# Gates of two batches made in one set of instructions, in an attention and mixture-of-experts kernel

## The chip, the cores and the metric

The kernel runs on one core of one Trainium2 chip. The metric is device time in microseconds (us), the median of several executions. The kernel before took 689.92 us in the median of three runs.

## What is computed

Two blocks, one behind the other. The first is attention with 8 batches, 8 heads, 576 positions and a head size of 64; heads 0 to 3 look at the last 32 positions, heads 4 to 7 at positions of the same class modulo 32. Its output, as rows `x` of 512 numbers (one for each of 8 x 576 positions), goes to a mixture of 8 experts. Each row is sent to one expert, and a gate decides which:

```
logits = np.einsum('bsd,de->bse', x, w_gate)
local_gate = 1.0 / (1.0 + np.exp(-np.einsum('bsd,de->bse', x, w_local).squeeze(-1)))
...
            fresh_e = int(np.argmax(logits[b, s]))
            if s == 0 or local_gate[b, s] < 0.5:
                e = fresh_e
            else:
                e = prev_e if prev_e >= 0 else fresh_e
            prev_e = e
            ls = logits[b, s] - logits[b, s].max()
            p = np.exp(ls)
            p /= p.sum() + 1e-09
            h = np.maximum(x[b, s] @ w1[e], 0.0)
            out[b, s] = p[e] * (h @ w2[e])
```

So each position needs nine numbers, 8 logits and the local gate, and from them a probability for each expert and a code that tells whether the expert is chosen afresh. All of it is in fp32.

## The kernel before, in words

The core has a matrix engine (TensorE, PE in the profile), a vector engine (VectorE, DVE), an activation engine (ScalarE, ACT), GpSimd (POOL) and SyncE (SP), which issues most of the DMAs. Each engine takes its instructions in the order of the program and waits on semaphores for others. [...] here the attention has three pools of PSUM tiles: `psS` (two tiles `sps`, for scores), `psV` (two tiles `vps`, for values and for gates) and `psT` (one tile `tps`, for transposes, for logits and for the router).

The order of the work is written out by hand in the loop at L433. Step `n` takes one pair of heads, in the order batch, pair (4 pairs a batch, so 32 pairs); a pair consists of two units. A step does, in this order: loads for four steps ahead (SP), scores and mask of pair n (L261, L265, L272), the store of finished rows of pair n-2 (L302), the transposes of pair n-2 (`turn_x`, L327), values and their normalizing for pair n-1 (L285, L298, L299), two of 16 weight sums for the first expert (L714, in steps 10 to 17, on DVE), and then what is due for whole batches. The last pair of batch b is number 4b+3; then

- `logits(b)` (L340) in step 4b+5: sixteen matmul records multiply the transposed rows by `wgs`, the weights of gate and local gate, padded to 32 columns. The four row blocks of 128 go to four strips of 32 rows of the tile `tps`, as four partial sums. Four copies (L351, L352, L354, L357) bring them to a tile `lT` of 128 partitions x 576 positions, two on ACT and two on DVE; the lower two also bring the positions of the strided heads back to their order. For batch 7 the engines of two copies change places and the tile is `sps`.
- `gates(b)` (L360) in step 4b+6: matmuls with a piece of `lT` as the stationary operand and `fold` as the moving one (L367) turn positions to partitions and add the four partial sums; there are 5 pieces, the last of 64 positions twice, so 6 matmuls, which the profile shows as 12 records. Thirteen small operations follow on 128 x 5 x 8 numbers (L372 to L392), all but one of them (L381, exp, on ACT) on DVE. They leave `codes` and `probs`.
- `store_p(b)` (L394) in step 4b+7: two DMAs from the POOL queue write the probabilities to DRAM beside the rows.

When four batches have their gates (step 19) the router for these starts: transposes of `codes`, scans on DVE (L547, L554), small matmuls (L559, L574) and a table. It takes one piece a step (`also[n]`), behind the gates in the same step. A gather of rows for the first expert is due in step 29. When the attention is done, the experts follow (L817, L853 and so on), to the end of the kernel; the change doesn't touch them.

Of the kernel before, what the change touches and what calls it, by code (L numbers as in the profile page):

```python
# [8 lines left out]
F32 = mybir.dt.float32  # L9
# [3 lines left out]
Alu = mybir.AluOpType  # L13
AX = mybir.AxisListType
# [4 lines left out]
P = 128  # L19
B, H, S, DH = 8, 8, 576, 64  # L20
D = H * DH
E, F = 8, 1024
DK, FK = D // P, F // P
# [14 lines left out]
PL, GC, GT = S // STRIDE, 7, 5  # L38
GR = STRIDE - GC * (GT - 1)
GK, GL = PL * GC, PL * GR  # L40
# [9 lines left out]
CH = -(-S // P)  # L50
RB = 4
# [7 lines left out]
WARM = 10  # L59

FILL = 4

ARMS = 7
SKIP = 8192
# [2 lines left out]
FRESH = -1.08674975e-07  # L67


def spread(ap, shape):  # L70

    dims = list("abcd"[:len(shape) - 1])
    left = " ".join(dims[:-1] + [f"({dims[-1]} o)"])
    right = " ".join(dims + ["o"])
    return ap.rearrange(f"{left} -> {right}", o=1).to_broadcast(shape)
# [7 lines left out]
def across(ap, shape):  # L83

    return ap.rearrange("a (o b) -> a o b", o=1).to_broadcast(shape)
# [60 lines left out]
def attention(ctx, tc, qkl, qks, vl, vs, wg, xd, ident, router, moe):  # L146

    nc = tc.nc
    sums, probs, codes = router.sums, router.probs, router.codes
    consts = ctx.enter_context(tc.tile_pool(name="consts", bufs=1))  # L150
# [4 lines left out]
    small = ctx.enter_context(tc.tile_pool(name="small", bufs=2))  # L155
# [4 lines left out]
    st = {}  # L160
# [18 lines left out]
    def busy(n):  # L179
        for _ in range(n):  # L180
            ps = psV.tile([P, 512], F32, name="vps")
            nc.tensor.matmul(ps, lhsT=warm[:, 0:P], rhs=warm, start=True, stop=True)  # L182

    busy(WARM)
    wgs = consts.tile([P, DK, 32], F32, name="wgs")
    nc.scalar.dma_start(out=wgs, in_=wg.rearrange("(k p) e -> p k e", p=P))

    identb = consts.tile([P, P], BF16, name="identb")
# [21 lines left out]
    for n, c in blocks:  # L210

        i, div = consts.tile([GK, 1], I32, name=f"row{n}"), consts.tile([GK, 1], F32, name=f"div{n}")
# [7 lines left out]
    n = GK  # L220
    nc.vector.tensor_copy(maskS[:, 0:2 * n].rearrange("p (a x) -> p a x", a=2), across(apart[n], [n, 2, n]))
    nc.vector.tensor_copy(maskS[:, 2 * n:], apart[GL])
    fold = consts.tile([P, E + 1], F32, name="fold")
    ci = consts.tile([P, E], I32, name="ci")
    down = consts.tile([P, E], F32, name="down")
    pi = consts.tile([P, CH], I32, name="pi")
    pos8 = consts.tile([P, CH], F32, name="pos8")
    start = consts.tile([P, CH], F32, name="start")

    def more_constants():  # L230

        nc.vector.tensor_reduce(fold, ident.rearrange("p (k x) -> p x k", k=DK)[:, 0:E + 1], axis=AX.X, op=Alu.add)


        nc.gpsimd.iota(ci, pattern=[[-1, E]], base=E, channel_multiplier=0)
        nc.vector.tensor_copy(down, ci)
        nc.gpsimd.iota(pi, pattern=[[E * P, CH]], base=E, channel_multiplier=E)
        nc.vector.tensor_copy(pos8, pi)
        nc.vector.tensor_scalar(start, pos8, float(E), None, Alu.is_equal)
# [100 lines left out]
    def logits(b):  # L340
        xT = st["xT", b]
        n = GK * (GT - 1)
        both = ((0, slice(0, n)), (1, slice(n, S)))
        final = b == B - 1

        ps = [psS.tile([P, 2, 512], F32, name="sps") for _ in range(2)] if final else [psT.tile([P, 2, 512], F32, name="tps")] * 2
        for kk, a, c in [(kk, *x) for kk in range(DK) for x in both] if final else [(kk, *x) for x in both for kk in range(DK)]:
            nc.tensor.matmul(ps[kk // 2][32 * kk:32 * kk + 32, a, 0:c.stop - c.start], lhsT=wgs[:, kk], rhs=xT[:, kk, c],  # L348
                             start=True, stop=True, skip_group_check=True)
        lT = small.tile([P, S], F32, name="lT")  # L350
        nc.scalar.copy(out=lT[0:64, 0:n], in_=ps[0][0:64, 0, 0:n])  # L351
        (nc.scalar.copy if final else nc.vector.tensor_copy)(out=lT[0:64, n:], in_=ps[0][0:64, 1, 0:GL])  # L352
        o = lT[64:].rearrange("p (y c) -> p y c", c=STRIDE)
        (nc.vector.tensor_copy if final else nc.scalar.copy)(  # L354
            out=o[:, :, 0:GC * (GT - 1)].rearrange("p y (j c) -> p j y c", c=GC),
            in_=ps[1][64:, 0, 0:n].rearrange("p (j y c) -> p j y c", j=GT - 1, c=GC))
        nc.vector.tensor_copy(o[:, :, GC * (GT - 1):], ps[1][64:, 1, 0:GL].rearrange("p (y c) -> p y c", c=GR))  # L357
        st["lT", b] = lT

    def gates(b):  # L360

        ps = psV.tile([P, 2, 3, V1], F32, name="vps").rearrange("p a i e -> p (a i e)")
        lt = ps[:, 0:CH * (E + 1)].rearrange("p (t e) -> p t e", e=E + 1)
        for t in range(CH):
            m = min(P, S - t * P)
            for o in range(0, P, m):
                nc.tensor.matmul(lt[o:o + m, t], lhsT=st["lT", b][:, t * P:t * P + m], rhs=fold,  # L367
                                 start=(t == 0), stop=True, skip_group_check=True)
        lg = lt[:, :, 0:E]
        shape = [P, CH, E]  # L370
        mx = small.tile([P, CH], F32, name="gmx")
        nc.vector.tensor_reduce(mx, lg, axis=AX.X, op=Alu.max)  # L372
        mxb = spread(mx, shape)
        ex = small.tile(shape, F32, name="ex")
        nc.vector.tensor_tensor(ex, lg, mxb, op=Alu.subtract)

        eq = small.tile(shape, F32, name="eq")
        nc.vector.tensor_tensor(eq, lg, mxb, op=Alu.is_equal)
        fr = small.tile([P, CH], F32, name="fr")
        nc.vector.scalar_tensor_tensor(fr, lt[:, :, E], FRESH, start, Alu.is_le, Alu.max)  # L380
        nc.scalar.activation(ex, ex, Act.Exp)  # L381
        nc.vector.tensor_tensor(eq, eq, across(down, shape), op=Alu.mult)
        code = small.tile([P, CH], F32, name="code")
        nc.vector.tensor_reduce(code, eq, axis=AX.X, op=Alu.max)
        nc.vector.tensor_tensor(code, pos8, code, op=Alu.subtract)

        nc.vector.tensor_tensor(codes[:, :, b], spread(code, shape), spread(fr, shape), op=Alu.mult)
        sm = small.tile([P, CH], F32, name="gsm")
        nc.vector.tensor_reduce(sm, ex, axis=AX.X, op=Alu.add)
        nc.vector.tensor_scalar(sm, sm, 1e-9, None, Alu.add)  # L390
        nc.vector.reciprocal(out=sm, in_=sm)
        nc.vector.tensor_tensor(probs[:, :, b, 0:E], ex, spread(sm, shape), op=Alu.mult)  # L392

    def store_p(b):  # L394
        dst = xd[b * S:(b + 1) * S, D:DX]
        full = S // P
        nc.gpsimd.dma_start(out=dst[0:full * P].rearrange("(t p) c -> p t c", p=P), in_=probs[:, 0:full, b])
        nc.gpsimd.dma_start(out=dst[full * P:], in_=probs[0:S - full * P, full, b])
# [19 lines left out]
    n = PAIRS * RB + 3  # L418
# [4 lines left out]
    m = n  # L423
# [9 lines left out]
    for n in range(len(units) + 3):  # L433
        if n < len(units):
            if n + ahead < len(order):
                load(*order[n + ahead])
            if 5 <= n < 13:
                moe.W[0].load(nc, moe.w1, moe.w2, 0, n - 5)
            if n == 10:
                steps = moe.W[0].sums(nc.vector)  # L440
            for u in units[n]:
                scores(u)
                mask(u)
        if 0 <= n - 2 < len(units) and order[n - 2][1] % 2 == 1:
            store_x(units[n - 2][1])
        if 0 <= n - 2 < len(units) and n != len(units):
            turn_x(*order[n - 2])
        if 0 <= n - 1 < len(units):
            for u in units[n - 1]:
                values(u)  # L450
                norm(u)
        if n == len(units):
            turn_x(*order[n - 2])
            moe.turn(moe.first, spare, 0)
        elif n == len(units) + 1:
            busy(FILL)
        for do in steps[:2]:
            do()
            steps.remove(do)
        for b in range(B):  # L460
            last = PAIRS * b + PAIRS - 1
            if n == last + 3:
                gates(b)
            if n == last + 4 and b < B - 1:
                store_p(b)
            if n == last + 2:
                logits(b)
        if n == len(units) + 1:
            moe.turn(moe.first, bank, 1)
            busy(2)  # L470
            moe.row_sums(moe.first)
        for do in also[n]:
            do()
# [1056 lines left out]
```

## Time and profile before

| | us |
|---|---|
| three timed runs | 687.54, 689.92, 690.97 |
| their median | 689.92 |
| the profiled execution | 686.27 |
| its span, first to last instruction | 684.5 |
| PE busy | 666.4 |
| DVE busy | 356.7 |
| ACT busy | 198.2 |

The attention ends and the first expert matmul begins at 165.0 us of the span. The granted clock of PE was 0.993 of full speed in the mean. A profile line of a group reads: line of the program, engine, operation, the tiles it writes and reads, shapes, count, then busy time, mean duration in ns, and the idle time of the engine just before with what ended it. A timeline line has start and duration first. A line of the chain of waits has start and duration and what the time went to. A line of the windows view has, for each stretch, its length, busy time and number of instructions of PE, PE's weight loads, DVE, ACT and POOL, then PE's granted clock, the share of the DMA engines and GB/s.

### The profile page before, as it was taken

To read this page: it belongs to the slowest core of one execution; us is meant where nothing else is said; L and a number is where in the kernel's file an instruction comes from. 1 tells how busy PE (TensorE), PEld (TensorE's weight loads), DVE (VectorE), ACT (ScalarE), POOL (GpSimd) and SP (SyncE) were. 2 spreads that over 40 slices of the span, in tenths; PEclk is the share of its full clock that TensorE was granted. 3 is DMA by queue.
4 is the path that set the end of the run, shared out by engine and by line. 5 is a ranking of instruction groups with operands and counts; after the bars stand their busy time and mean duration, and the time that the engine had idled before them with its cause. 6 is when DMAs were issued, how large, how long until landed. Compare 5 with 4: busy or idle time off the path is not lost.

```text
span 684.5 us, 14864 instructions
## 1 busy us (share of the span) xinstructions
PE 666.4 (97%) x6055; PEld 574.2 (84%) x6056; DVE 356.7 (52%) x821; ACT 198.2 (29%) x365; POOL 117.7 (17%) x144
## 2 busy tenths in 40 slices
PE   9999999999999999999999999999999999999994
PEld 6888887887998999589989999997799899699493
DVE  6558866865895437126532654651256546522131
ACT  3454453544312221222222122122222132221220
POOL 3440000012021113111111202202111113121001
PEclk9999999999999999999999999999999999999998
DMA  9999878733611172171236118111612622021001
GB/s 322 402 377 329 274 250 279 255 114 121 226 36 43 50 268 76 40 275 40 57 120 204 56 29 294 51 32 40 251 48 65 234 75 72 34 57 41 18 9 35
DMA packets 35800, 95.80 MB, mean 140 GB/s; under 512 B 4790, under 2 KB 11702, under 8 KB 35628
## 3 DMA queue, kind: packets, MB, share of 16 engines
q1 hardware_dynamic: 27164, 71.41, 29.6%
q0 software_dynamic: 7936, 22.38, 10.1%
q8 instruction: 66, 1.08, 0.6%
q14 instruction: 106, 0.87, 0.4%
q10 hardware_dynamic: 528, 0.07, 0.1%
HBM read 74.66 MB, written 19.69 MB: 138 GB/s over the span
## 4 chain that ended last, share of the span: by engine, by line
PE 93%; DVE 3%; issue 1%; ACT 1%; DMA 1%; POOL 0%; SPq 0%; DVEq 0%; POOLq 0%
PE lps L817 30%; PE mps L853 28%; PE sps L261 6%; PE vps L285 5%; PE lps L908 4%; PE mps L919 4%; PE tps L327 3%; PE xps L760 2%; PE mps L949 2%; PE lps L929 2%; PE sps L255 2%; PE vps L367 1%; PE tps L348 1%; DVE xl L299 1%; PE vps L182 1%
## 5 line engine op out<-in xcount | busy, mean ns | idle before, releaser
L773 POOL DMA_INDIRECT out_dram<-y,tab x40 | 46.1, 1153 | 351.4 <-DVE y L805 247.4
L817 PE MATMUL lps<-tt,ws 128*128 128x128 f32 x768 | 91.8, 275 | 0.3 <-issue 0.3
L817 PEld LDWEIGHTS lps<-tt,ws 128*128 128x128 f32 x768 | 88.6, 192 | 0.6 <-issue 0.5
L853 PE MATMUL mps<-wt,k 128*128 128x256 f32 x384 | 85.7, 380 | 0.0
L853 PEld LDWEIGHTS mps<-wt,k 128*128 128x128 f32 x384 | 72.8, 190 | 9.9
L817 PE MATMUL lps<-xt,w1t 128*128 128x128 f32 x512 | 63.2, 276 | 3.0 <-ACT y L955 1.9
L817 PEld LDWEIGHTS lps<-xt,w1t 128*128 128x128 f32 x512 | 60.4, 192 | 6.5 <-ACT y L955 3.7
L805 DVE TENSOR_TENSOR h<-lps,u 128x512 f32<-128x512 f32 x48 | 33.2, 691 | 58.3 <-PE lps L817 58.2
L853 PE MATMUL mps<-w2t,h 128*128 128x256 f32 x256 | 60.5, 379 | 0.0
L747 POOL DMA_INDIRECT x<-xd,gi x40 | 41.1, 1027 | 84.8 <-issue 34.7
L265 ACT ACTIVATE e<-sps 128x576 f32<-128x576 f32 (+1 forms) x64 | 41.3, 650 | 40.0 <-PE sps L261 39.2
L853 PEld LDWEIGHTS mps<-w2t,h 128*128 128x128 f32 x256 | 47.4, 190 | 5.8
L261 PE MATMUL sps<-qk 64*128 64x96 f32 (+2 forms) x704 | 51.2, 283 | 0.1
L804 ACT ACTIVATE h<-h 128x512 f32<-128x512 f32 x48 | 30.3, 630 | 70.1 <-DVE h L805 69.0
L261 PEld LDWEIGHTS sps<-qk 64*128 64x128 f32 (+2 forms) x704 | 43.1, 185 | 8.5 <-issue 7.2
L804 ACT ACTIVATE h<-lps 128x512 f32<-128x512 f32 (+1 forms) x28 | 15.7, 563 | 81.8 <-PE lps L817 65.6
L805 DVE TENSOR_TENSOR u<-lps,p 128x512 f32<-128x512 f32 x16 | 11.1, 691 | 52.5 <-PE lps L817 31.6
L753 ACT ACTIVATE x<-x 128x512 f32<-128x512 f32 (+1 forms) x40 | 27.1, 717 | 34.5 <-DMA x<-xd,gi 21.1
L761 ACT COPY xt<-xps 128x512 f32<-128x512 f32 (+1 forms) x38 | 20.3, 565 | 49.3 <-PE xps L760 49.3
L817 PE MATMUL lps<-xt,ws 128*128 128x128 f32 x256 | 31.3, 275 | 0.0
L817 PE MATMUL lps<-tt,w1t 128*128 128x128 f32 x256 | 31.3, 275 | 0.0
L853 PE MATMUL mps<-w2t,k 128*128 128x256 f32 x128 | 30.4, 380 | 0.0
(236 smaller groups left out, 974.5 us busy)
## 6 DMA issues: line engine op xcount, KB each, us to landing
w1t<-in_w_dram SPq DMA_DIRECT2D x7, 2048.0 KB
w2t<-in_w_dram SPq DMA_DIRECT2D x7, 2048.0 KB
qk<-in_qkl_dram SPq DMA_DIRECT2D x16, 592.0 KB
qk<-in_qks_dram SPq DMA_DIRECT2D x16, 576.0 KB
vl<-in_vf_dram SPq DMA_DIRECT2D x8, 780.0 KB
vs<-in_vg_dram SPq DMA_DIRECT2D x8, 639.8 KB
xd<-xl SPq DMA_DIRECT2D x12, 288.0 KB
xd<-xs SPq DMA_DIRECT2D x48, 63.0 KB
```

The costliest lines, as they stand in the source:

```text
L261: nc.tensor.matmul(ps[0:m, h, c:c + w], lhsT=t[r, S + j * width:S + j * width + m], rhs=t[r, j * width:j * width + w], start=(u.local and ...
L265: nc.scalar.activation(e[0:kb, :, 0:n], ps[0:kb, :, 0:n], Act.Exp, bias=0.0, scale=1.0 / DH ** 0.5)
L285: nc.tensor.matmul(ps[a * HALF:(a + 1) * HALF, h, i], lhsT=u.e[0:m, h, q0:q0 + HALF], rhs=vt[0:m, j, 2 * i2 + h], start=(i == 0 and h == 0 ...
L747: self.nc.gpsimd.indirect_dma_start(out=r.x[0:r.m, i], out_offset=None, in_=self.xd[0:r.rows], in_offset=bass.IndirectOffsetOnAxis(ap=r.gi ...
L753: self.nc.scalar.activation(r.x[0:r.m, i, 0:D], r.x[0:r.m, i, 0:D], Act.Copy, scale=r.gate[i][0:r.m])
L773: s = self.nc.gpsimd.indirect_dma_start(out=self.out, out_offset=bass.IndirectOffsetOnAxis(ap=r.si[i][0:r.m], axis=0), in_=y[0:r.m, i], in ...
L804: relu = lambda o, i: nc.scalar.activation(o, i, Act.Relu)
L805: add = lambda o, i, p: nc.vector.tensor_tensor(o, p, i, op=Alu.add)
L817: nc.tensor.matmul(ps[:, f], lhsT=m[:, kk, f * P:(f + 1) * P], rhs=v[:, kk], start=(start and f == 0 and kk == 0), stop=(kk == 1), skip_gr ...
L853: nc.tensor.matmul(ps[:, 0:256], lhsT=m[:, f], rhs=v[:, f], start=(start and f == 0), stop=(f == 3), skip_group_check=True)
L908: nc.tensor.matmul(ps[:, f], lhsT=w.w1[:, kk, c:c + P], rhs=r.xt[:, 0, kk], start=(f == 0 and kk == 0), stop=(kk == DK - 1), skip_group_ch ...
L919: nc.tensor.matmul(ps, lhsT=h[f // 4][:, f % 4], rhs=w.w2[:, f], start=(f == 0), stop=(f == FK - 1))
```

## The change

The gates of batches 0 and 1, 2 and 3, and 4 and 5 are made by one call each (`TWINS` is {1: 0, 3: 2, 5: 4}); batches 6 and 7 stay alone. For this the weights `wgs` get 16 columns of zeros ahead of them. The first of two batches uses columns 16 to 47, so its logits lie in rows 0 to 8 of each strip of 32, with zeros below; the second uses columns 0 to 31, so its logits lie in rows 16 to 24. Instead of copying the second's, four additions on DVE add them to the first's `lT` in place. `gates` is not called after the first of two; after the second it is called once, with 18 columns of `fold` for 9, and its small operations work on 80 numbers a partition for 40. Both batches' `store_p` come in the step behind it. The matmuls of `logits`, the copies of first and single batches and the places of the calls are as they were.

```diff
+TWINS = {b: b - 1 for b in range(1, B - 1, 2) if b % RB}
...
-    wgs = consts.tile([P, DK, 32], F32, name="wgs")
+    wgs = consts.tile([P, DK, 48], F32, name="wgs")
...
-        nc.vector.tensor_reduce(fold, ident.rearrange("p (k x) -> p x k", k=DK)[:, 0:E + 1], axis=AX.X, op=Alu.add)
+        nc.vector.tensor_reduce(fold, ident.rearrange("p (k x) -> p x k", k=DK), axis=AX.X, op=Alu.add)
...
+        second = b in TWINS
+        w = slice(0, 32) if second else slice(16, 48)
...
-            nc.tensor.matmul(ps[kk // 2][32 * kk:32 * kk + 32, a, 0:c.stop - c.start], lhsT=wgs[:, kk], rhs=xT[:, kk, c],
+            nc.tensor.matmul(ps[kk // 2][32 * kk:32 * kk + 32, a, 0:c.stop - c.start], lhsT=wgs[:, kk, w], rhs=xT[:, kk, c],
...
+        if not second:
+            st["lT", b] = small.tile([P, S], F32, name="lT")
+        lT = st["lT", b] = st["lT", TWINS.get(b, b)]
...
+        for i, (to, of) in enumerate(parts):
+            if second:
+                nc.vector.tensor_tensor(to, of, to, op=Alu.add)
+            elif i == (1 if final else 2) or i == 0:
+                nc.scalar.copy(out=to, in_=of)
+            else:
+                nc.vector.tensor_copy(to, of)
...
-        lt = ps[:, 0:CH * (E + 1)].rearrange("p (t e) -> p t e", e=E + 1)
+        lt = ps[:, 0:CH * n * (E + 1)].rearrange("p (t b e) -> p t b e", b=n, e=E + 1)
+        to = fold.rearrange("p (b x) -> p b x", b=2)[:, 0:n, 0:E + 1]
...
-                nc.tensor.matmul(lt[o:o + m, t], lhsT=st["lT", b][:, t * P:t * P + m], rhs=fold,
+                nc.tensor.matmul(lt[o:o + m, t], lhsT=st["lT", b][:, t * P:t * P + m], rhs=to,
...
-            if n == last + 3:
+            if n == last + 3 and b + 1 not in TWINS:
                 gates(b)
-            if n == last + 4 and b < B - 1:
-                store_p(b)
+            if n == last + 4 and b < B - 1 and b + 1 not in TWINS:
+                for both in {TWINS.get(b, b), b}:
+                    store_p(both)
```

## The prediction

> **What bounds the kernel now.** I read the page first, for the engine totals and the clock, then the chain of work that ended last, in order of time, over the attention stage (0 to 165 us, where all of the change lies), then the timeline around the steps that the diff touches, then groups by form for durations.
>
> ```profile
> PE 666.4 (97%) x6055; PEld 574.2 (84%) x6056; DVE 356.7 (52%) x821; ACT 198.2 (29%) x365; POOL 117.7 (17%) x144
> ```
>
> TensorE (PE) is busy all through, so a saved instruction counts only if PE would have run it with no gap to fill. The chain around the gates of batch 0 shows that:
>
> ```profile
> 30.69 0.87 PE vps L285 x24
> 31.58 0.21 DVE sums L298
> 31.81 0.56 DVE xl L299
> 32.37 0.12 DVE sums L298
> 32.52 1.25 PE vps L367 x12
> 33.77 0.36 PE sps L255 x2
> ```
>
> The 12 gate matmuls (L367) take 1.25 us and the next scores (L255) follow at once. Before them PE stands idle a little: L367 takes a buffer of the two `vps`, which comes free only when VectorE (DVE) has read the values just made (L298, L299). So a call of `gates` costs PE its matmuls and that gap. The next view is the timeline at batch 1's logits, PE's matmuls up to 46.46 us:
>
> ```profile
> 46.53 0.57 ACT L351 COPY lT<-tps 64x504 f32<-64x504 f32 x1 [1.99 <-PE tps L348]
> ...
> 47.13 0.23 DVE L352 COPY lT<-tps 64x72 f32<-64x72 f32 x1 [0.94 <-ACT lT L351]
> ...
> 47.39 0.61 ACT L354 COPY lT<-tps 64x504 f32<-64x504 f32 x1 [0.29 <-DVE lT L352]
> ...
> 48.03 0.24 DVE L357 COPY lT<-tps 64x72 f32<-64x72 f32 x1 [0.67 <-ACT lT L354]
> ...
> 48.57 0.87 PE L327 MATMUL tps<-ident,xl 128*128 128x128 f32 x6
> ```
>
> The four copies out of `tps` run one after the other over two engines, 46.53 to 48.27. The next transposes (L327) write the same single buffer, so they need the last copy done; here PE comes at 48.57 anyway. At batch 3 it is the copies that are late:
>
> ```profile
> 84.52 1.28 DVE L714 TENSOR_TENSOR wt<-w2t,wt 128x512 f32<-128x512 f32 x2
> ...
> 86.61 0.24 DVE L357 COPY lT<-tps 64x72 f32<-64x72 f32 x1 [0.67 <-ACT lT L354]
> ...
> 87.00 0.85 PE L327 MATMUL tps<-ident,xl 128*128 128x128 f32 x6 [0.34 <-DVE lT L357]
> ```
>
> PE waits 0.34 us, because DVE had two weight sums (L714) in its queue first. Last, the windows view: PEclk, the last number before the DMA share, is 1.00 everywhere in attention except one window.
>
> ```profile
> 107.98:111.39 3.41, 2.83 (x50) 2.50 (x48) 2.53 (x10) 0.24 (x1) 0.00 (x0) 1.00 0.30 92
> 111.39:114.81 3.42, 3.42 (x25) 2.63 (x23) 2.49 (x13) 1.16 (x2) 1.32 (x2) 0.50 0.83 264
> ```
>
> The window at half clock follows the one in which PE was least busy, and that one holds the gates of batch 4 with a longer gap.
>
> [...]
>
> ```profile
> L805 DVE TENSOR_TENSOR u<-lps,p 128x512 f32<-128x512 f32 x4 | 2.8, 690 | 8.4 <-PE lps L817 8.4
> ...
> L354 DVE COPY lT<-sps 64x504 f32<-64x504 f32 x1 | 0.7, 685 | 3.6 <-PE sps L348 3.6
> ```
>
> **Part 1, gates of batches 0, 2 and 4 removed from PE.** Value matmuls of a local pair take 1.55 us in the chain where scores follow directly (25.05 to 26.60). Batch 0: they start at 30.69, would end at 32.24, the scores start at 33.77: 1.53 us saved. Batch 2: 68.64 + 1.55 = 70.19 against 71.72: 1.53. Batch 4: values start at 107.22 (chain time), end at 108.77; next is the router's L559, at 110.60: 1.83. L559 needs the scan `cum`, done at 108.39 (107.04 + 1.35), and the `tps` copy done at 107.90, so neither takes the place of the wait. Sum 4.89 us, all on the path: PE has no other gap there and the scores behind need loads and buffers that are ready.
>
> Loads: the `qk` and `vl`/`vs` packets end 7 us or more before their first use from 28 us on (4.7 kB and 4.6 kB packets of `qk`, for instance: those of batch 1's last pair end at 26.5, wanted at 34.1), though the DMA engines are full until 60 us; 3 us of speed-up are covered. Tightest for DVE: the fourth `w1t` piece ends at 49.6 (its semaphore about 50.2), the first L714 starts at 51.74 and would move to 50.2. If it waits there, up to 1 us is hidden by DVE's idle 1.0 us at 55.2; behind it are only gate operations, for which PE does not wait.
>
> **Part 2, gates of 1, 3 and 5 widened.** L367 streams 18 columns instead of 9. L574 streams 32 with 12 records in 1.24 us (116.63 to 117.86), the pace of 9. So 0; at worst the slope up to L817, whose 32 records of 128 columns took 3.77 us in the chain (118 ns): 14 ns over 119 columns, so 9 columns in 12 records are 0.013 us a call. DVE and ACT operate on 80 elements instead of 40: about 40 ns in each of seven, 0.3 us a call, hidden by the idle 1.0 us of DVE after the gates of 1; after those of 5 an L298 comes 0.1 us late (136.0), and PE wants its buffer at 138.8. Were that cover gone, each call would cost its 0.3.
>
> **Part 3, adds instead of copies for 1, 3 and 5.** Two copies leave ACT (0.57 and 0.61 us), four adds stand on DVE; only the first waits, for PE. L714 shows the pace of two such adds: 1.28 for two of 0.68, so 0.60 each while another follows; a 72-column one adds 0.14. Chain: 0.60 + 0.14 + 0.60 + 0.24 = 1.58 us, against 1.74 for the copies when DVE is free. No row shows an add whose one operand is the strided (y, c) pattern; its copy is L354's 685 ns, so I take the same, and as bounds 0.57 (nothing is below the 504 elements at the measured pace) and 1.2 us (double).
> - Batch 1: 46.53 + 1.58 = 48.11, PE comes at 48.57: 0.
> - Batch 3: DVE is free at 85.72, chain ends at 87.30, PE 0.15 later, as now: 87.45 against 87.00. Costs 0.45.
> - Batch 5: DVE is busy with L299 until 126.95; the chain ends at 128.53, PE starts at 128.66 against 128.36. Costs 0.30. The router's L620 (1.2 and 0.27 us), queued behind the adds, ends by 130.0; the next L298 comes at 130.13.
>
> With the bound of 1.2 us the chain is 2.78, and the costs are 0.9, 1.65 and 1.5: 4.05.
>
> **Part 4, small.** `store_p` of 0, 2, 4 moves behind 1, 3, 5 on POOL: two more issues of 0.79 and 0.56 us, before a POOL that is idle till 74, 113 and 149 us; SP's queue is not passed. The rows are read first by the gather at 149.21. `wgs` (96 KB for 64, wanted at 26.5 us) and `fold` (0.21 us of DVE at 11.7, about 0.1 longer, before 2 us idle): 0.
>
> **Sum.** 4.89 - 0.75 = 4.14 us. The profiled execution took 686.27 (span 684.5 and 1.8 around), so 682.1 for it at its clock. Its time is below all three timed runs (687.54 to 690.97), so I take the gain from their median: 689.92 - 4.14 = 685.8. About 0.5% (3.4 us) is what a measurement of this kernel can tell from no change; the threshold is 686.5.
>
> **Rivals.**
> - *The slow clock window goes too.* In the half-clock window scores and transposes took 0.91, 0.73, 1.38 and 1.11 us where 0.64, 0.42, 0.76 and 0.81 are usual: 1.5 us. Without the gates of batch 4 the weak stretch 108.77 to 110.81 is gone. For: it follows exactly that stretch. [...] 4.14 + 1.5 = 5.6, so 684.3.
> - *DVE takes over from PE.* From 75 to 87 us the chain runs over DVE back to back (L299, L714, L272). If DVE's work there, not PE, sets the time, batch 2's gates give nothing: 4.14 - 1.53 = 2.6, so 687.3. Against: DVE was idle 1.02 us at 74.4, waiting for PE, so it shifts with PE.
> - *The adds hold `tps` (slower).* Stall over the three sites: 3 x (t - 1.58) + 0.44, t being the add chain. It eats 4.89 us at t = 3.06, a long add of 1.34 us; from there the kernel is slower. At 2.0 us per long add t is 4.38, the stall 8.84: 693.9. Nothing in the profile has DVE at 4 ns per element.
>
> The compiled order shows that the change does what it says: three sets of gates fewer, four adds in three places.
>
> **Numbers.** Forecast 0.52, clock window 0.22, DVE 0.20, adds 0.06. The forecast's own spread is about 1 us either way (median of few runs, the pace of adds), so three quarters of it lie beyond 0.5%: faster 0.52 x 0.75 + 0.22 = 0.61, same 0.13 + 0.20 = 0.33, slower 0.06. Range: from 683.0 (clock window and noise) to 688.4 (DVE case and noise, or adds at 1.0 us).
>
> **What would show it.** Right: PE goes from L285 to L255 with no gap at batches 0 and 2 and to L559 at 4; the four adds end 1.6 us after they start; L327 waits 0.8 us for them at batch 3, 0.3 at 5, none at 1; the first expert matmul comes about 4 us earlier than 165.0. Wrong: long adds of over 0.8 us, `qk` waits on PE, or new half-clock windows.

## The result, and the profile after

The changed kernel took 684.28 us in the median of 6 runs (683.26 to 686.79), the kernel before beside it 690.36: ratio 0.9927, 95% interval 0.9900 to 0.9954. A second measurement gave 685.13 (9 runs) against 690.27 (54 runs): 0.9939, 0.9919 to 0.9960. By the ratios the change makes the kernel 4 to 5 us faster (5.1 to 6.1 by the medians); forecast were 4.14 and 685.8.

The profiled execution took 684.04 us, with a span of 682.3 and a granted clock of 0.994. First the engine totals of the changed kernel (the weight loads have fallen by 36, the records of three calls):

```profile
PE 662.7 (97%) x6020; PEld 570.5 (84%) x6020; DVE 355.5 (52%) x791; ACT 194.2 (28%) x356; POOL 117.5 (17%) x144
```

Lines have moved: the scores are L258 and L264 (before L255, L261), the values L288 (L285), the transposes L330 (L327), the additions L366, the gate matmuls L382 (L367), the weight sums L732 (L714), the router's small matmul L577 (L559), the experts L835 (L817).

TensorE's lines of the timeline at the values of batch 0 (second line: PE goes on to the scores with nothing between), and at those of batch 4, where the router's L577 now follows at once:

```profile
30.44 1.62 PE L288 MATMUL vps<-vl,e 128*64 128x65 f32 x48
31.99 0.43 PE L258 MATMUL sps<-maskS,identb 126*126 126x252 bf16 x2
```
```profile
104.68 1.62 PE L288 MATMUL vps<-vl,e 128*64 128x65 f32 x48
106.23 0.22 PE L577 MATMUL tps<-cum,same 32*32 32x1 f32 x2
106.44 0.43 PE L258 MATMUL sps<-maskS,identb 126*126 126x252 bf16 x2
```

From the start of the values to the next matmul it is 1.55 us in both places. Before it was 3.08 (30.62 to 33.70) at batch 0 and 3.38 (107.15 to 110.53) at batch 4.

The timeline at the logits of batches 1, 3 and 5 (two, three and two lines, others left out): the four additions, and the transposes that need `tps`.

```profile
44.82 1.66 DVE L366 TENSOR_TENSOR lT<-tps,lT 64x504 f32<-64x504 f32 x4 [0.34 <-PE tps L354]
...
46.86 0.87 PE L330 MATMUL tps<-ident,xl 128*128 128x128 f32 x6
```
```profile
81.57 1.28 DVE L732 TENSOR_TENSOR wt<-w2t,wt 128x512 f32<-128x512 f32 x2
...
82.77 1.66 DVE L366 TENSOR_TENSOR lT<-tps,lT 64x504 f32<-64x504 f32 x4
...
84.58 0.85 PE L330 MATMUL tps<-ident,xl 128*128 128x128 f32 x6 [0.93 <-DVE lT L366]
```
```profile
121.12 1.65 DVE L366 TENSOR_TENSOR lT<-tps,lT 64x504 f32<-64x504 f32 x4
...
122.92 0.85 PE L330 MATMUL tps<-ident,xl 128*128 128x128 f32 x6 [0.31 <-DVE lT L366]
```

The chain takes 1.66 us (forecast 1.58). Batch 1 waits for nothing; batch 3 waits 0.93 us behind the two weight sums that stand ahead on VectorE; batch 5 waits 0.31. The widened gate call costs what the narrow one did:

```profile
49.56 1.26 PE L382 MATMUL vps<-fold,lT 128*128 128x18 f32 x12 [0.28 <-DVE sums L301]
```

By the start of batch 6's values the changed kernel is 5.47 us ahead (143.51 against 148.98). But the first expert matmul starts at 162.31 against 165.00, only 2.7 us ahead, and the spans differ by 2.2. What is lost lies at the gates of batch 6. TensorE's lines there, first before, then in the changed kernel:

```profile
148.98 1.62 PE L285 MATMUL vps<-vl,e 128*64 128x65 f32 x48
150.94 1.25 PE L367 MATMUL vps<-fold,lT 128*128 128x9 f32 x12 [0.35 <-DVE sums L298]
```
```profile
143.51 1.73 PE L288 MATMUL vps<-vl,e 128*64 128x65 f32 x48
146.74 1.25 PE L382 MATMUL vps<-fold,lT 128*128 128x9 f32 x12 [1.49 <-PE vps L288]
```

Before, the gates came 1.96 us after the start of the values, here 3.23: 1.27 us late, because the values themselves report their end late: VectorE's first read of them (L301, before L298) starts 2.29 us after their start, before 1.03. The windows view shows what follows. The first line is the window behind the old place of batch 4's gates, the others are the two around batch 6's gates; the number ahead of the DMA share is the clock.

```profile
108.15:111.57 3.42, 3.42 (x66) 3.11 (x62) 1.83 (x5) 1.35 (x2) 0.00 (x0) 1.00 0.44 124
145.16:148.57 3.41, 1.92 (x19) 1.65 (x20) 2.01 (x8) 0.07 (x1) 0.91 (x1) 1.00 0.65 171
148.57:151.98 3.41, 3.41 (x25) 2.62 (x22) 1.47 (x10) 1.33 (x3) 1.38 (x2) 0.50 0.66 163
```

The half-clock window that stood behind batch 4's gates is gone, and a new one stands behind the weak stretch at batch 6. So the two profiles differ by 4.0 us of the change itself (the sum of its steps, worked out below), 0.2 of the start and, by difference, about 1.3 of the lost window (together 5.5 at batch 6), less 1.27 of the late end, about 1.5 of the new window and 0.5 among the experts. Whether the late end is a price of the change was the first question for the runs.

### The profile page after: what moved, and what is told of

Read it like the earlier page. It is cut to its first block, busy times and chain, and to the rows that moved or that the text cites. A ratio compares the mean times of both kernels' runs of the same rounds, so it can differ in the third digit from the quotient of the medians.

```text
span 682.3 us, 14753 instructions
## 1 busy us (share of the span) xinstructions
PE 662.7 (97%) x6020; PEld 570.5 (84%) x6020; DVE 355.5 (52%) x791; ACT 194.2 (28%) x356; POOL 117.5 (17%) x144
## 4 chain that ended last, share of the span: by engine, by line
PE 57%; issue 1%; DVE 1%; DMA 1%; ACT 0%; POOL 0%; POOLq 0%; ACTq 0%
PE lps L835 22%; PE mps L871 21%; PE mps L937 4%; PE lps L926 3%; PE mps L967 2%; PE lps L947 2%; PE xps L778 2%; DMA x<-xd,gi 1%; PE lps L957 0%; DVE h L958 0%; ACT y L973 0%; POOL out_dram L791 0%; DVE wt L732 0%; DVE y L823 0%; ACT x L771 0%
## 5 line engine op out<-in xcount | busy, mean ns | idle before, releaser
L835 PE MATMUL lps<-tt,ws 128*128 128x128 f32 x768 | 91.8, 275 | 0.6 <-issue 0.6
L835 PEld LDWEIGHTS lps<-tt,ws 128*128 128x128 f32 x768 | 88.6, 192 | 1.0 <-issue 0.8
L835 PE MATMUL lps<-xt,w1t 128*128 128x128 f32 x512 | 63.2, 277 | 3.0 <-ACT y L973 1.9
L835 PEld LDWEIGHTS lps<-xt,w1t 128*128 128x128 f32 x512 | 60.4, 192 | 6.5 <-ACT y L973 3.7
L264 PE MATMUL sps<-qk 64*128 64x96 f32 (+2 forms) x704 | 51.2, 282 | 0.5 <-issue 0.4
L264 PEld LDWEIGHTS sps<-qk 64*128 64x128 f32 (+2 forms) x704 | 43.0, 185 | 8.8 <-issue 7.4
L835 PE MATMUL lps<-tt,w1t 128*128 128x128 f32 x256 | 31.3, 275 | 0.0
L835 PE MATMUL lps<-xt,ws 128*128 128x128 f32 x256 | 31.3, 275 | 0.0
```

The source lines that it names most:

```text
L264: nc.tensor.matmul(ps[0:m, h, c:c + w], lhsT=t[r, S + j * width:S + j * width + m], rhs=t[r, j * width:j * width + w], start=(u.local and ...
L835: nc.tensor.matmul(ps[:, f], lhsT=m[:, kk, f * P:(f + 1) * P], rhs=v[:, kk], start=(start and f == 0 and kk == 0), stop=(kk == 1), skip_gr ...
```

## The experiments

Theories: T1, the gain is the gate matmuls taken off TensorE less the waits behind the additions. T2, windows of half clock add to or take from that. T3, the gain is VectorE's relief from three sets of small operations, and the matmuls count little. T4, T5 and T6 came up on the way and are explained in their place. Each ratio is to the kernel before, run on the same chip beside it.

**The gate matmuls of batches 0, 2 and 4 back on TensorE, read by nobody.**

```
+            if n == last + 3 and b + 1 in TWINS:
+                again(b)
```

Here `again` holds the 6 matmuls of `gates` for one batch, with 9 columns, into a `vps` tile.

> The changed kernel, with the 6 gate matmuls (12 records) of batches 0, 2 and 4 put back on PE in their old places, into a vps tile that nobody reads; their small operations on DVE and ACT stay away. Theory 1 (the gain is PE's own time of the three sets of matmuls and the gap before them, less the stalls of the adds): 4.6 to 4.9 us come back, so 0 to 1 us slower than the kernel before, ratio to before about 1.000 to 1.002. Theory 2 (part of the gain is fewer windows at half clock behind the weak stretches of the gates): the same, and the mean clock falls back to that of the kernel before. Theory 3 (the gain is the relief of DVE and ACT): at most 1 us comes back, ratio about 0.993.

Measured: 690.06 us (14 runs), ratio 0.9997 [0.9971, 1.0023]. The whole gain is gone, although all small operations stay paired. The three calls (L417 there) waited 0.28, 0.28 and 0.64 us and ran 1.25 each: 4.95 us. Their line in the summary of TensorE's waits (us in total, times, longest):

```profile
PE vps L417 <- DVE sums L301: 1.2, 3, 0.6
```

T3 as the main cause falls. One part of the expectation missed: the mean clock did not fall back (below, at the table).

**The small operations of batches 0, 2 and 4 back on VectorE and ScalarE, on a constant tile, read by nobody.**

```
+            if n == last + 3 and b + 1 in TWINS:
+                again(b)
```

Here `again` holds the 13 operations of `gates` for one batch, on 40 numbers a partition of a constant tile.

> The changed kernel, with the thirteen small operations of batches 0, 2 and 4 put back on DVE and ACT in their old places, on a constant in SBUF and into scratch tiles; no gate matmuls with them. Theory 1: DVE has idle time there, so at most 0.3 us over the changed kernel; ratio to before 0.992 to 0.995. Theory 3: half the gain or more is gone, ratio 0.996 or above.

Measured: 685.88 us (15 runs), 0.9940 [0.9915, 0.9964]: by the ratio nearly the whole gain stays, as expected. But it isn't free, and the 0.3 us over the changed kernel that T1 allowed were too little: the medians of the changed kernel are 0.8 and 1.6 us lower. One new wait appears at batch 4, where the operations stand ahead of the router's reads (L606) of the one tile `tps`:

```profile
110.25 0.87 PE L332 MATMUL tps<-ident,xl 128*128 128x128 f32 x6 [1.21 <-DVE total L606]
```

The waits behind the additions also grow, from 1.2 us in sum to 1.6. So the matmuls carry the gain, and without VectorE's relief some 1.6 us of it would go into waits again.

**The additions issued ahead of the weight sums** (pairs, adds first).

```
+        for b in TWINS:
+            if n == PAIRS * b + PAIRS + 1:
+                logits(b)
         for do in steps[:2]:
...
-            if n == last + 2:
+            if n == last + 2 and b not in TWINS:
                 logits(b)
```

> The changed kernel, with the logits of batch 3 put ahead of the two weight sums of that step in DVE's queue; PE's order is as it was. Theory 1 with the stall of the transposes at batch 3 due to DVE's queue: the wait of 0.93 us before them goes to 0.1 or less and the attention ends 0.8 us earlier, at equal clock windows; timed 0.8 us below the changed kernel, ratio to before about 0.991. Theory 3 or a stall that is hidden: no change, and what is late next (the value matmuls or the norm) keeps the time.

Measured: 682.24 us (6 runs), 0.9877 [0.9834, 0.9920]; span 681.5 against 682.3. The timeline at batch 3, now with the sums (L735) behind the additions:

```profile
82.00 1.65 DVE L366 TENSOR_TENSOR lT<-tps,lT 64x504 f32<-64x504 f32 x4
...
83.68 1.29 DVE L735 TENSOR_TENSOR wt<-w2t,wt 128x512 f32<-128x512 f32 x2
...
84.00 0.87 PE L330 MATMUL tps<-ident,xl 128*128 128x128 f32 x6
```

No bracket stands behind the transposes: the 0.93 us are gone, and the span shows 0.8 of them. The median fell by more than the 0.8 expected, 2.0 us; the rest goes with the clock of these six runs, 0.9942 in the mean against 0.9915 in the first six of the changed kernel (worth about 1.4 us by the line below).

**Four more reads of `tps` ahead of the additions**, to lengthen the chain by some 2.7 us at each place (four of 504 columns at about 0.68).

```
+        if second:
+            for _ in range(2):
+                nc.vector.tensor_copy(junk[0:64, 0:n], parts[0][1])
+                nc.vector.tensor_copy(o[:, :, 0:GC * (GT - 1)].rearrange("p y (j c) -> p j y c", c=GC), parts[2][1])
```

> The changed kernel, with four more long reads of tps on DVE (into scratch) ahead of the adds at batches 1, 3 and 5, so that the chain that holds tps is about 4.3 us in place of 1.66. The sum of the prediction (stall = 3 x (t - 1.58) + 0.44) gives 8.6 us of stall, 7.9 us more than in the changed kernel: 3.7 us slower than before, ratio about 1.005. Theory 2 adds half-clock windows after the waits of 2.4 to 3.2 us: up to 1.5 us each, so up to 1.011. If PE had other work to hide the waits, the ratio would stay at 0.993 to 1.000.

Measured: 700.49 us (6 runs), 1.0164 [1.0111, 1.0217]. The waits of TensorE, from the same summary:

```profile
PE tps L331 <- DVE lT L372: 9.4, 3, 3.8
```

The prediction's formula, 3 x (t - 1.58) + 0.44 with t = 1.58 + 2.72, gives 8.6 of waiting. The time rose by more than the waits: 16.2 us above the changed kernel, and beyond the 1.011 that the expectation took for the worst case. The granted clock of the profile fell to 0.978, with a half-clock stretch behind each of the three waits, of 3.41, 3.41 and 13.65 us. T2 holds here, and was priced too low: each of these waits, of 2.5 to 3.8 us, was followed by half clock on top of its length (the values behind the first took 2.87 us for 1.62).

**The kernel before, unchanged, profiled a second time, and the changed kernel, unchanged.**

> The kernel before, unchanged, for a second profile of it. T1 (the gain is the gate matmuls less the stalls behind the adds): 688 to 692, and the values of batch 6 that are followed by a gate call on TensorE come to their end about 0.96 us after their start, as in the first profile of before, so that the late end seen there in all the changed kernels (about 1.3 us) is a cost of the change. T4 (that late end belongs to this place of the program and comes and goes between executions): it shows here too, 1.3 to 1.5 us of wait at the gates of batch 6, and then it is no part of the change's price.

> The changed kernel, unchanged, with more runs. T1: ratio to before 0.993 to 0.9945 (4.1 to 5 us), since the sum of the prediction was 4.14 and the first measurement gave 5.0 by the ratio. T2 (a part of the gain is half-clock windows that come more seldom): the mean granted clock of its runs lies above that of before by 0.001 to 0.003, and runs of both with the same clock differ by 4 to 5 us.

Measured: before 690.44 (18 runs), after 685.13 (9 runs), 0.9939 [0.9919, 0.9960] to the 690.27 of the runs beside both. The timeline of before at batch 6, second profile:

```profile
149.47 1.62 PE L285 MATMUL vps<-vl,e 128*64 128x65 f32 x48
...
152.72 1.54 PE L367 MATMUL vps<-fold,lT 128*128 128x9 f32 x12 [1.62 <-remote]
```

The gates come 3.25 us after the values' start, as in the changed kernel. So the late end belongs to this place in both kernels (T4); the first profile of before happened to have none. It doesn't come from the change. Two profiles can't tell whether it is as frequent before; the table below leaves little room for a price of 1.3 us. This pair of profiles has spans of 688.7 and 681.0, a difference of 7.7 where the first pair shows 2.2: one pair of spans can't size a gain of 4. Much of it is the clock: this profile of before has 10.2 us at half clock ahead of the kernel's tail, this one of the changed kernel none.

The runs also split the gain. The table gives the mean time of all runs of the two kernels in these measurements, by granted clock (132 runs of before from three of the measurements here, 15 of after from two); at the same clock they differ by 3.6 to 4.0 us, apart from 0.995 with its one run.

| clock | before, us (runs) | after, us (runs) |
|---|---|---|
| 0.990 | 690.1 (12) | 686.1 (5) |
| 0.991 | 688.6 (5) | 684.6 (2) |
| 0.992 | 688.4 (6) | 684.4 (4) |
| 0.994 | 687.8 (10) | 684.2 (2) |
| 0.995 | 686.6 (7) | 685.1 (1) |
| 0.997 | 686.4 (14) | 682.8 (1) |

The mean clock of after was 0.9923 in this measurement, that of before 0.9905. A line through the runs of before falls by 0.53 us per 0.001 of clock, so 0.0018 is worth 1.0 us. So about 3.8 us come at equal clock, from less work, and 1 us goes with the higher clock (estimates from this line).

The same line corrects the first two runs. With the matmuls put back the mean clock was 0.9916, against 0.9898 in the runs of before beside it; T2 had expected it to fall back. At equal clock that kernel is then about 0.7 us slower than before (690.06 + 1.0 against 690.33), inside T1's 0 to 1. So the 1 us of clock isn't tied to the gate matmuls, and its cause stays open. With the small operations put back the clock was 0.9936, worth 2.0 us; without these, about 2.4 us of gain are left of the 3.8, which fits the 1.6 us of added waits.

**Gates of three batches together** (0 to 2 and 4 to 6, shifts of 9 and 18 rows), alone and with the additions first.

```
-TWINS = {b: b - 1 for b in range(1, B - 1, 2) if b % RB}
+TWINS = {1: 0, 2: 0, 5: 4, 6: 4}
...
-        w = slice(0, 32) if second else slice(16, 48)
+        low = 2 * (E + 1) - (b - TWINS.get(b, b)) * (E + 1)
+        w = slice(low, low + 32)
```

> Gates of batches 0 to 2 and 4 to 6 made together, the shifts 9 and 18 rows; four gate calls instead of five. T1: one call of 1.25 us less on TensorE; batch 3 copies again, so its stall of 0.93 goes; batches 2 and 6 get adds, and pay 0.3 to 0.9 each where their sums or the last norm stand ahead on VectorE. Together 0.4 to 1.9 us less than the pairs, ratio to before 0.991 to 0.993. Rival (VectorE has no room left: three times the small operations in one block at batches 2 and 6 hold up what stands behind them): no gain over the pairs, ratio 0.994 or more.

> The threes, and in the batches that add the logits are issued ahead of the weight sums, as in the pairs' variant that gained 0.8 in the profile's span. T1: 0.3 to 1.2 us less than the threes alone, ratio to before 0.986 to 0.991. Rival (what counts in these runs is the number of half-clock windows, not the stall): within 0.3 us of the pairs with the adds first, 0.9877.

Measured: 691.26 us (22 runs), 1.0031 [1.0013, 1.0048], and 690.01 (14 runs), 1.0006 [0.9986, 1.0026]. Both expectations missed: one gate call less, and the time is that of before. Neither VectorE nor the stall at batch 3 is the main reason. Near 240 us the threes alone were 0.5 us ahead of the second profile of the pairs (239.26 against 239.76 at the same matmuls), and the threes with the adds first 0.4 behind theirs (240.93 against 240.53); then TensorE stops twice in the midst of the experts, far from the change (threes alone; the second version stops there 3.15 and 2.31 us):

```profile
241.86 1.05 PE L836 MATMUL lps<-xt,w1t 128*128 128x128 f32 x8
246.07 1.87 PE L836 MATMUL lps<-xt,w1t 128*128 128x128 f32 x8 [3.15 <-issue]
```
```profile
296.23 1.49 PE L836 MATMUL lps<-xt,w1t 128*128 128x128 f32 x11 [0.47 <-ACT y L974]
299.88 0.84 PE L836 MATMUL lps<-xt,w1t 128*128 128x128 f32 x5 [2.15 <-issue]
```

"issue" means that nothing the profile shows was waited for, and the stop falls inside a group of 16 equal matmuls. Among the DMA packets there are some of a queue called "instruction". In both versions one of 16 KB starts 0.7 to 0.8 us after TensorE has stopped at the first place (243.62 and 245.37), and TensorE goes on 2.4 us behind its start (246.07 and 247.74). At the second place they start at 297.32 and 297.76, just before the stops, and it goes on 2.5 us later. Hence T5, a guess from these times: TensorE had run out of instructions, and with 12 matmul records fewer than the pairs the next ones came at a bad moment.

**The same with 12 TensorE instructions more at the start, and the control with the pairs.** Four of ten warm-up matmuls of 512 columns are cut into four of 128 each: no more columns, only more instructions.

```
-    busy(WARM)
+    busy(WARM - 4)
+    for _ in range(4):
+        ps = psV.tile([P, 512], F32, name="vps")
+        for c in range(0, 512, P):
+            nc.tensor.matmul(ps[:, c:c + P], lhsT=warm[:, 0:P], rhs=warm[:, c:c + P], start=(c == 0), stop=True,
```

> The threes with the adds first, and four of the ten warm-up matmuls of 512 columns at the start cut into four of 128 each: the same columns, 12 TensorE instructions more, nothing else. T5 (the threes lost 3.15 and 2.2 us at two places among the experts because TensorE's instructions, being fewer, are fetched at other moments, behind the weights' transfers): with the count of the pairs back, both waits go, and the time falls from 690.0 to 684 to 681.5, a ratio of 0.987 to 0.991. Rival (the threes are late for some dependency of the data): the waits and the time stay, 1.0006.

> The control: the pairs with the adds first, with the same cut of the warm-up, so 12 TensorE instructions more than the version that took 682.24. T5 expects no new wait among the experts, since the kernel before has 36 more at that place and shows none: 0.9877 within 0.002. If the position of the fetches decides at any shift, a wait of 2 to 3 us turns up somewhere and the ratio is 0.991 or more.

Measured: the threes 683.07 us (8 runs), 0.9909 [0.9876, 0.9943]; the pairs 685.12 (18 runs), 0.9952 [0.9932, 0.9973]. With twelve instructions more, the threes are 6.9 us faster, and both stops are gone. All waits for "issue" in the threes' summary, before the padding and after it:

```profile
PE lps L839 <- issue: 6.6, 4, 3.2
```
```profile
PE lps L844 <- issue: 1.1, 2, 0.6
```

T5's first part holds, as far as waits and time show it. Its second part, that the pairs wouldn't care, does not: the control lost 2.9 us against the unpadded 682.24, and shows a new stop of 1.06 at 61.25; its waits for "issue" sum to 3.6 us against 2.0 without padding, which is most of the 1.9 us between the spans (683.4 and 681.5). So twelve TensorE instructions at the start of the program, of no weight themselves, move the time by 3 to 7 us, and how much of it stands in a comparison of two of these versions can't be read from their diff.

The change itself removes 36 such records, so this is a rival for its gain. The profiles settle it: the waits of TensorE for "issue" sum to 1.4 and 1.3 us in the two profiles of before, 2.1 and 1.7 in those of the changed kernel, and 1.5 with the matmuls put back. Such stops take 0.3 to 0.8 us from the gain; they don't make it.

**The first gather moved on GpSimd**, one step and two steps later (T6), from the pairs with the adds first. The gather starts 0.24 us into the values of batch 6, the ones that end late.

```
-    also[m + 5].append(lambda: moe.gather(moe.first))
+    also[m + 6].append(lambda: moe.gather(moe.first))
```

The second of these kernels has `m + 7`.

> The pairs with the adds first, and the first gather issued one step of the units later on GpSimd. T6 (the late end of batch 6's values comes from that gather, which starts 0.24 us into them in every profile): the wait at the gates of batch 6, 1.5 to 1.9 us, goes; if the gather hurts wherever it falls, a wait of that size appears one step later instead. 0.3 to 1.9 us less than the pairs with the adds first, ratio 0.985 to 0.9875. Rival (the wait belongs to this place of TensorE's program, whatever GpSimd does): it stays, 0.9877.

> The edit of the gather issued one step later left the gather where it was, since GpSimd had been waiting for something else; here it is issued two steps later, behind the store of batch 6's gates on the same queue, which waits for those gates. T6 (the late end of batch 6's values comes from the gather that starts 0.24 us into them): the gates of batch 6 come without the wait of 1.5 to 1.9 us, and the gather, now at about 151, delays the scaling of its rows and the first transposes of them by 1 to 3 us, so that the time gains little, 0.986 to 0.992. Rival (the late end belongs to that place of TensorE's program, whatever GpSimd does): the wait stays, and the time is 1 to 3 us above the pairs with the adds first.

Measured: one step, 682.29 us (13 runs), 0.9900 [0.9876, 0.9925], with the gather at the same place (142.63, values at 142.39) and the wait of 1.68 in place: GpSimd had been waiting for a transpose anyway (11.34 us), so this tested nothing, but is a second measurement of the pairs with the adds first. Two steps, 684.78 (15 runs), 0.9930 [0.9910, 0.9949]: the gather starts at 150.20, and the gates of batch 6 come 1.90 us after the values' start. That is just outside the 0.986 to 0.992 that T6 expected, and 2.5 us above the pairs with the adds first. TensorE's lines of that kernel, and then where it waits instead:

```profile
142.81 1.62 PE L288 MATMUL vps<-vl,e 128*64 128x65 f32 x48
144.71 1.25 PE L382 MATMUL vps<-fold,lT 128*128 128x9 f32 x12 [0.28 <-DVE sums L301]
```
```profile
PE sps L781 <- ACT x L774: 1.6, 1, 1.6
PE tps L330 <- ACT xT L334: 1.5, 1, 1.5
```

T6 is supported, not shown: with the gather beside them, the values ended late in all profiles but the first one of before; without it, in the one profile there is, they don't. How a gather would delay them stays open. The move doesn't pay: TensorE waits 1.6 us for the scaling of the gathered rows (L774) instead.

## Why the prediction was right

**Part 1, matmuls removed: right.** Forecast 1.53, 1.53 and 1.83 us; from the start of the values to the next matmul it is now 1.55 at all three places (before 3.08 at batch 0), and putting the matmuls back took the whole gain.

**Part 2, widening: right.** 12 records of 18 columns take 1.26 us against 1.25. The eight small operations of VectorE on 80 numbers take 228 to 243 ns for 188 to 201, about 41 ns more each (forecast 40, for seven with ScalarE's; there are nine with its one), and TensorE waits for none of them.

**Part 3, additions: right in mechanism, a little low in size.** The chain is 1.66 us for 1.58: the 72-element additions take 222 ns, the long ones 677 in the mean (those with the strided operand 685 to 686, the others 664 to 675; VectorE's copy of that size had taken 685). Forecast stalls 0, 0.45 and 0.30 more than before; measured 0, 0.59 (0.93 for the 0.34 of before) and 0.31. The sum is 0.90 for 0.75, so 4.89 - 0.90 = 3.99 by the steps, and 3.6 to 4.0 by runs at equal clock. The rival that turns the sign needed a chain of 3.06 us; the run with four more reads showed that it exists and that the formula is a fair one (8.6 for a measured 9.4), but that it leaves out the half clock behind such waits.

**Part 4, moved stores and constants: right as far as seen.** No wait on them appears in the changed kernel.

**The clock.** The rival with 5.6 us (the window behind batch 4's gates goes) happened in the first profile, and that window came back, at 113.04 us, in the profile with the matmuls put back. But a new one stood behind batch 6. Over many runs the clock gave about 1 us, so the result lies between the forecast and this rival; since the mean clock didn't fall when the matmuls came back, this us is not the one that the rival argued, and to that extent the larger gain was luck. The half-clock stretches ahead of the kernel's tail are 3.41 us long in the first profile of both kernels, 3.41, 3.41 and 13.65 behind the lengthened waits, and 10.2 in all in the second profile of before. In the two first profiles the stretch came behind one in which TensorE was weak: busy for 2.83 of 3.41 us in before, for 1.92 in the changed kernel. Not every weak stretch brings one: the second profile of the changed kernel has the wait of 1.6 us at batch 6 and no half clock behind it.

**VectorE as the bound, 687.3: wrong.** Batch 2's matmuls gave their 1.53 us, and the lead was still there behind the stretch in question: 2.94 us at the scores behind batch 2's values (68.71 against 71.65), 2.42 behind the stall at batch 3 (85.35 against 87.77).

**A sign that misled.** "The first expert matmul about 4 us earlier" came out as 2.7. The step was right; the profile of before that it was measured against lacked the late end at batch 6 that all others with that gather have, and the changed one had a half-clock window behind it. And the forecast took its stalls and gaps as a fixed ground: it had no term for stops like those of the padded runs, worth 3 to 7 us there. That no stop of this size met the changed kernel was luck.

The fastest version is the pairs with the additions first: 682.24 and 682.29 us in two measurements, some 8 us below the kernel before and 2 to 3 below the changed one. Of the latter, 0.9 is the stall at batch 3. The threes with padding may have less work still: their median (683.07) doesn't show it, but their clock was 0.9912 in the mean against 0.9942 and 0.9938, which by the line above is worth about 1.5 us.

## What to carry to other kernels

When one engine is busy all through, price a change by what leaves that engine's path and by the waits that the new work puts on it, place by place: here that gave 3.99 us by the steps where 4.14 were forecast. Check where the new operation stands in its queue: moving it ahead of work that nobody waits for removed the largest stall, 0.93 us, and no cost of it was seen. Compare many runs and more than one profile before a gain below 1% is put down to a cause, for half-clock stretches (10.2 us of them in one profile of before, none in one of the changed kernel) and the stops for "issue" (6.6 us in sum in one version) moved the time by as much as this gain.

## What the runs showed of the hardware

- TensorE stopped for 2.15 to 3.15 us in the midst of equal matmuls, and went on 2.4 to 2.6 us after the start of a 16 KB instruction packet; twelve more instructions at the start of the program removed the stops and changed the time from 690.01 to 683.07, and the same padding made another version slower, 682.24 to 685.12. That TensorE had run out of instructions and waited for the fetch is inferred from packet times and from these shifts, not seen.
- The spread between runs of one kernel goes with the clock: 0.53 us per 0.001 of mean granted clock. One window of 3.41 us at half clock is 0.0025 of the mean (1.71 of 690), so about 1.3 us (an estimate); the runs of before reached from 0.981 (694.6 us) to 0.997 (686.4).
- Where an indirect gather on GpSimd started inside a group of value matmuls, the end of that group was reported 1.2 to 2.4 us late in 12 of 13 profiles (the gates behind it came 3.2 to 4.3 us after the group's start, against 1.96 in the thirteenth and 1.90 in the one profile without the gather there). The cause is not shown.
